# A fused Hyena filter and maxout FFN: the w_out product two steps behind, and another load table for the VectorE work between

## The chip, the cores and the metric

One core of a Trainium2 chip runs the whole kernel. The metric is device time in microseconds of one execution; several executions of each kernel are timed, and the median is compared. The engines of the core run side by side, each with its own in-order queue, and wait for each other by semaphores: TensorE (PE, matmuls; PEld its weight loads), VectorE (DVE), ScalarE (ACT), GpSimd (POOL) and SyncE (SP, which here issues DMAs only).

## The reference

A long convolution (by FFT) along the sequence, gated by the input, and then a feed-forward block whose hidden value is the maximum of three products:

```python
def _attn_ref(x, v, pos_emb, w1, w2):
    B, S, D = x.shape                                  # 4, 12544, 128
    h_mlp = np.maximum(pos_emb @ w1, 0.0) @ w2
    h_filt = h_mlp * np.exp(-0.01 * pos)[:, None]
    u = x * v
    L = 2 * S
    Uf = np.fft.rfft(u, n=L, axis=1)
    Hf = np.fft.rfft(h_filt, n=L, axis=0)
    y = np.fft.irfft(Uf * Hf[None], n=L, axis=1)[:, :S, :]
    return x * y

def _moe_ref(x, w1, w2, w3, w_out):                    # x: 50176 x 128, d_ff 768
    h = np.maximum(np.maximum(x @ w1, x @ w2), x @ w3)
    return h @ w_out
```

All of it is float32.

## The kernel before

The convolution of one batch is a three-stage transform made of small matmuls; the FFN of one batch takes its result from DRAM. A prologue computes the filter's spectrum and the first batch's convolution. Then comes the loop that the change touches: while the FFN of batch b runs (b = 0, 1, 2), the convolution of batch b+1 is spread between its steps. A last part does the FFN of batch 3 alone, in another form.

*The FFN.* A batch is 32 tiles (`NT`) of 392 columns, and d_ff is 6 steps (`NF`) of 128 rows. w1 has been subtracted from w2 and w3 beforehand, and its part is applied as one 128x128 matrix `lin`, so that step f of a tile is: `up` (L689) makes `pa = w_sb[1]ᵀ g`, ScalarE writes `hid = relu(pa)` (L694), `pb = w_sb[2]ᵀ g`, and VectorE writes `hid = max(hid, pb)` (L697). `down` (L700) adds `wo_sb[f]ᵀ hid` into the accumulator `ops`; in step 0 it first starts that accumulator with `lin`, in step 5 ScalarE copies it to `ot` (L710) and POOL issues the output DMA (L712). Each of `pa`, `pb`, `lin` and one `ops` product is four matmul instructions on two column halves of the array.

Buffers: `pa` and `pb` take turns through three PSUM banks (`hps`, 3 buffers); `ops` is one bank; `hid` has 3 buffers, `ot` 2, `gt` 3.

*The next tile.* `t_load` (L634) loads its transformed data `zt` and the gate `xT`, two tiles ahead. `t_sums` (L658) makes a sum and a difference, in step 1: on POOL (L662, L663), but on VectorE (two L666) for tiles of the upper half of batches 1 and 2. `t_last` (L670), in step 3, does the last transform stage (`yps`) and the gating (`gt`, L684).

*The convolution between.* `conv_steps` (L572) hands out its work to the 192 slots (32 tiles of 6 steps) of a batch's FFN. For u in 0..31 come loads, a product, a transpose and the first stage (`u_first`). Then 45 pairs of frequencies (`NK`) go through the middle: products with 64x64 weights (`g_quarter`, `psq`, L462 and L472, in slot s; it also does the third stage of the pair three before, from its `xs`), `g_fold` in slot s+1 (ScalarE copies half of `psq` to `eo`, L484, VectorE adds and subtracts, L487), `q_swap` in s+2 and s+3 (two ScalarE copies each, L502, L503), then `q_re` (VectorE, L506), `q_im` (VectorE L511, then POOL L514) and two `q_unfold` (VectorE, L518) in the slots that `emptiest` picks by the table `load`, and at the end `g_store` (POOL DMA, L495). `per_pair`, the distance of two pairs, is 2.67 slots in the first batch and 2.53 in the others, so the pairs fall differently on the six steps of a tile.

*The order.* Nothing reorders: the program's order is each engine's order. Within one step the loop emits `t_load` (step 0), `t_sums` (step 1), `up` of this step, `down` of the step before, `t_last` (step 3), and then what `conv_steps` put into the slot; `q_swap`, `g_fold` and the rest in the order of their pairs, `g_quarter` and `u_first` last. So `ot` of a tile stands, on ScalarE, after the first activation of the next tile and ahead of the swaps and the fold of its slot 0; on POOL its output DMA stands ahead of the next `t_sums`.

Of the kernel before, what the change touches and what calls it, by code (L numbers as in the profile page):

```python
# [89 lines left out]
def kernel(  # L90
# [59 lines left out]
    def halves_mm(out, lhsT, rhs, start, stop):  # L150


        for h in range(2):
            nc.tensor.matmul(out[64 * h:64 * h + 64], lhsT[:, 64 * h:64 * h + 64], rhs,  # L154
                             start=start, stop=stop, skip_group_check=True)
# [416 lines left out]
    def conv_steps(b, done):  # L572


        out = []

        def at(slot, late, fn, *args):
            out.append((slot, late, len(out), fn, args))

        per_pair = 170 / (NK + LATE + 0.6 * (NU - done))
        for u in range(done, NU):
            s = (u - done) * 0.6 * per_pair + 9
            at(max(0, int(s) - 9), 0, u_load, b, u)
            at(int(s) - 6, 0, u_mul, u)
            at(int(s) - 5, 0, u_planes, u)
            at(int(s) - 4, 0, u_dma, u)
            at(int(s), 0, u_join, u)
            at(int(s + 1), 1, u_first, u)  # L590
        s0 = int((NU - done - 1) * 0.6 * per_pair + 9) + 6
        load = [(1.2 if i % NF == 3 else 0.6) + (1.4 if i % NF == 1 and b > 1 and i >= NT * NF // 2 else 0)
                for i in range(NT * NF)]
        for x in range(NK + LATE):
            load[s0 + int(x * per_pair) + 1] += 1.4

        def emptiest(among, cost):
            s = min(among, key=lambda i: load[i])
            load[s] += cost
            return s  # L600

        for x in range(NK + LATE):
            s = s0 + int(x * per_pair)
            g, z = x if x < NK else None, x - LATE if x >= LATE else None
            at(s, 1, g_quarter, g, z)
            at(s + 1, 0, g_fold, g, z)
            at(s - 4, 0, w_load, x)
            if z is not None:
                at(s + 3, 0, g_store, b, z)
            if g is None:  # L610
                continue
            if g % 2 == 0:
                at(s - 4, 0, q_load, g, min(2, NK - g))
                at(s - 1, 0, h_load, g, min(2, NK - g))
            at(s + 2, 0, q_swap, g, 0)
            at(s + 3, 0, q_swap, g, 64)
            last = s0 + int((x + LATE) * per_pair) - 1
            a = emptiest(range(s + 4, min(s + 5, last - 2) + 1), 0.7)
            at(a, 0, q_re, g)
            a = emptiest(range(a, min(s + 6, last - 1) + 1), 0.7)  # L620
            at(a, 0, q_im, g)
            for q in range(2):
                at(emptiest(range(a + 1, last + 1), 0.55), 0, q_unfold, g, q)
        slots = {}
        for s, _, _, fn, args in sorted(out, key=lambda r: r[:3]):
            slots.setdefault(s, []).append((fn, args))
        return slots
# [6 lines left out]
    def t_load(b, i):  # L634
        zt = hp.tile([N1, 2, 512], FP32, tag="zt", name="zt", bufs=2)
        for c in range(2):
            if b == 0:
                nc.sync.dma_start(
                    zt[NK * c:NK * c + NK],
                    zd[b].rearrange("(g a) c t f -> g a c t f", a=2)[  # L640
                        :, :, c, 2 * i:2 * i + 2, :].rearrange("g a t f -> g a (t f)"))
                continue
            q, j = divmod(i, NT // 2)
            for a in range(2):
                nc.sync.dma_start(
                    zt[NK * c:NK * c + NK, a].rearrange("g (t f) -> g t f", t=2),
                    zd[b].rearrange("(g a) c t q f -> g a c t q f", a=2)[
                        :, a, c ^ (a & q), 2 * j:2 * j + 2, q, :])
        zts[b, i] = zt[:, 0], zt[:, 1]
        if i % 2:  # L650
            return
        xT = hp.tile([D, 2, 4, NB], FP32, tag="xT", name="xT", bufs=2)
        for c in range(GC):
            nc.sync.dma_start(xT[c * NG:(c + 1) * NG].rearrange("d i p n -> d (i p) n"),
                              x[:, 4 * i:4 * i + 8, c, b, :])
        xTs[b, i], xTs[b, i + 1] = xT[:, 0], xT[:, 1]

    def t_sums(i, eng=nc.gpsimd):  # L658
        z0, z1 = zts[i]
        even = hp.tile([N1, 512], FP32, tag="even", name="even", bufs=2)  # L660
        if i[0] == 0 or i[1] < NT // 2:
            eng.tensor_tensor(out=even[:], in0=z0, in1=z1, op=ALU.add)  # L662
            eng.tensor_tensor(out=z1, in0=z0, in1=z1, op=ALU.subtract)  # L663
        else:
            for out, op in ((even[:], ALU.add), (z1, ALU.subtract)):
                nc.vector.scalar_tensor_tensor(out=out, in0=z1, scalar=sign_t[:, 0:1], in1=z0,  # L666
                                               op0=ALU.mult, op1=op)
        zts[i] = even[:], z1

    def t_last(i):  # L670
        zt = zts.pop(i)
        ps = cps.tile([P, state["yps"]], FP32, tag="cv", name="yps")
        own = i[0] == B - 1 and i[1] > 1
        g = (lp if own else hp).tile([D, 4, NB], FP32, tag="g", name="gt", bufs=4 if own else 3)
        y = ps[:, 0:N].rearrange("d (p n) -> d p n", p=4)

        h = NB // 2
        for s in range(4):
            for a in range(2):
                halves_mm(y[:, s, a * h:a * h + h], zt[a][:, s * D:(s + 1) * D],  # L680
                          f4p[:, i[0] > 0 and i[1] >= NT // 2, a, :], s == 0 and a == 0, True)
        y = y.rearrange("d p (a m) -> d p m a", a=2)
        xT = xTs.pop(i)
        nc.vector.tensor_tensor(out=g[:].rearrange("d p (m a) -> d p m a", a=2), in0=y,  # L684
                                in1=xT.rearrange("d p (m a) -> d p m a", a=2),
                                op=ALU.mult)
        gs[i] = g
# [12 lines left out]
    def down(i, f, h):  # L700
        if f == 0:
            pos_[i] = ops.tile([D, 512], FP32, tag="ops", name="ops")
            halves_mm(pos_[i][:, 0:N], lin[:], gs[i][:].rearrange("d p n -> d (p n)"), True,
                      False)
        halves_mm(pos_[i][:, 0:N], wo_sb[:, f, :], h[:], False, f == NF - 1)
        if f < NF - 1:
            return
        gs.pop(i)
        o = op_.tile([D, 4, NB], FP32, tag="o", name="ot")
        nc.scalar.copy(o[:].rearrange("d p n -> d (p n)"), pos_.pop(i)[:, 0:N])  # L710
        dst = outT.rearrange("d (p b n) -> d p b n", b=B, n=NB)[:, 4 * i[1]:4 * i[1] + 4, i[0], :]
        nc.gpsimd.dma_start(dst, o[:])  # L712
# [94 lines left out]
    def run(steps):  # L807
        for fn, args in steps:
            fn(*args)
# [216 lines left out]

    tiles = [(b, i) for b in range(B) for i in range(NT)]
    LAST = (B - 1) * NT
    late = None
    for n, (b, i) in enumerate(tiles[:LAST]):  # L1030
        if i == 0:
            beside = {}
            beside = conv_steps(b + 1, EARLY if b == 0 else 0)
        if n == 0:
            t_load(*tiles[0])
            t_load(*tiles[1])
            t_sums(tiles[0], nc.vector)
            t_last(tiles[0])
        for f in range(NF):

            if i < NT - 2:
                if f == 0:
                    t_load(*tiles[n + 2])
            elif i == NT - 1 and f < 2 and n + 1 + f < len(tiles):
                t_load(*tiles[n + 1 + f])
            turn_ = i == NT - 1
            if f == (3 if turn_ else 1):
                t_sums(tiles[n + 1], nc.vector if turn_ else nc.gpsimd)
            if f == 4 and n + 1 == LAST:
                t_sums(tiles[n + 2], nc.vector)  # L1050
            h = up((b, i), f)
            if late is not None:
                down(*late)
            late = ((b, i), f, h)
            if f == (4 if turn_ else 3):
                t_last(tiles[n + 1])
            if f == 5 and n + 1 == LAST:
                t_last(tiles[n + 2])
            s = i * NF + f
            run(beside.pop(s, ()))  # L1060
            if s == NT * NF - 1:
                assert not beside, sorted(beside)
    first = up((B - 1, 0), 0)
    down(*late)
    conv.close()


# [20 lines left out]
    step, b = 0, B - 1  # L1088
    for i in range(0, NT, 2):
        h = {}  # L1090
# [63 lines left out]
```

## Time and profile before

| | us |
|---|---|
| median of 6 runs | 2351.21 |
| lowest and highest | 2348.91, 2354.92 |
| the profiled execution, its time | 2354.92 |
| its span, first to last instruction | 2353.1 |

Granted TensorE clock over the span: 0.994 of full speed. Busy time by stretch, in us, with the DMA engines' share (packet times over 16 engines, which can exceed 1):

| stretch | what runs | PE | DVE | ACT | POOL | DMA |
|---|---|---|---|---|---|---|
| 0 to 340 | prologue, first convolution | 316.8 | 235.6 | 219.9 | 108.5 | 0.72, 0.82 |
| 340 to 990 | FFN of batch 0 and some of 1 | 648.0 | 436.0 | 333.8 | 279.2 | 0.90 |
| 990 to 1460 | FFN of batch 1 and some of 2 | 461.7 | 325.1 | 255.4 | 158.5 | 0.88 |
| 1460 to 1930 | FFN of batch 2 | 461.5 | 332.9 | 258.2 | 159.9 | 0.86 |
| 1930 to 2353 | FFN of batch 3 | 412.4 | 198.4 | 105.2 | 268.4 | 0.22 |

A line of a list of groups or waits reads: line of the kernel, engine, operation, written<-read tiles. In a timeline, each row is a run of equal instructions: start, length, engine, line, operation, tiles, how many, and in brackets the engine's idle time before it and what ended it. The end of a matmul is modelled, so rows of TensorE overlap; the distance of starts is the safer measure.

### The profile page before, as it was taken

How to read it: one execution, taken by the hardware profiler on the slowest of the kernel's cores; microseconds unless marked ns; L12 is line 12 of the kernel's file. 1: busy time of each engine (PE TensorE's matmuls, PEld its weight loads, DVE VectorE, ACT ScalarE, POOL GpSimd, SP SyncE). 2: the span in 40 equal slices, each digit the busy share in tenths (PEclk: the TensorE clock that was granted, in tenths of full speed). 3: DMA queues.
4: the chain of work that ended last, by engine and by line, in shares of the span. 5: the costliest groups of instructions: out<-in, count | busy, mean ns of one | idle time of the engine just before them, and what ended most of it. 6: DMA issues, size and time to landing. Idle time of an engine off the chain costs nothing.

```text
span 2353.1 us, 67998 instructions
## 1 busy us (share of the span) xinstructions
PE 2300.4 (98%) x27853; PEld 1374.3 (58%) x27853; DVE 1528.1 (65%) x2798; ACT 1172.4 (50%) x2124; POOL 974.6 (41%) x1153
## 2 busy tenths in 40 slices
PE   8999989999999999999999999999999999999998
PEld 7988866655545446654454446655454546666665
DVE  4678857757777747757787747757777755444443
ACT  2678844456666624446666624446666622222222
POOL 1045414334444434334332324434333326666666
PEclk9999999999999999999999999999999999999999
DMA  6868959979898859979989849969899932222221
GB/s 149 209 201 263 288 148 186 167 175 229 224 241 218 209 124 191 185 142 239 229 233 239 223 111 194 185 145 243 223 228 244 228 81 70 57 54 66 68 54 22
DMA packets 473145, 410.92 MB, mean 175 GB/s; under 512 B 328004, under 2 KB 374231, under 8 KB 472834
## 3 DMA queue, kind: packets, MB, share of 16 engines
q1 hardware_dynamic: 433504, 317.61, 61.2%
q0 software_dynamic: 26400, 75.72, 11.1%
q10 hardware_dynamic: 12930, 13.25, 1.8%
q8 instruction: 219, 3.59, 0.7%
q14 instruction: 92, 0.75, 0.1%
HBM read 262.77 MB, written 84.67 MB: 148 GB/s over the span
## 4 chain that ended last, share of the span: by engine, by line
PE 80%; DMA 8%; ACT 4%; issue 3%; DVE 3%; SPq 1%; POOL 1%; ACTq 0%; POOLq 0%; DVEq 0%
PE pa L154 20%; PE pb L154 19%; PE ops L154 16%; PE ops L757 6%; PE ps L408 5%; PE yps L154 5%; PE psq L462 3%; PE ps L163 3%; PE psq L472 2%; DMA hd<-ht 2%; DMA wt<-wq_const 1%; DMA zt<-zd 1%; DMA sq<-spec 1%; ACT ht L949 1%; PE pm L323 1%
## 5 line engine op out<-in xcount | busy, mean ns | idle before, releaser
L694 ACT ACTIVATE hid<-pa 128x392 f32<-128x392 f32 x768 | 383.1, 499 | 683.5 <-PE pa L154 658.0
L697 DVE TENSOR_TENSOR hid<-hid,pb 128x392 f32<-128x392 f32 x768 | 428.3, 558 | 425.5 <-PE pb L154 332.3
L154 PE MATMUL pa<-gt,w_sb 128*64 128x392 f32 x3072 | 648.3, 499 | 0.8 <-DVE gt L684 0.8
L154 PE MATMUL pb<-gt,w_sb 128*64 128x392 f32 x3072 | 638.9, 493 | 3.7 <-ACT hid L694 3.7
L154 PE MATMUL ops<-hid,wo_sb 128*64 128x392 f32 x2304 | 478.9, 493 | 15.6 <-DVE hid L697 15.6
L154 PEld LDWEIGHTS pb<-gt,w_sb 128*64 128x64 f32 x3072 | 223.4, 137 | 288.2 <-issue 270.8
L514 POOL TENSOR_TENSOR cb<-cb,xs 128x512 f32<-128x512 f32 x135 | 174.7, 1294 | 445.2 <-DVE xs L511 167.7
L154 PEld LDWEIGHTS ops<-hid,wo_sb 128*64 128x64 f32 x2304 | 165.8, 137 | 232.5 <-issue 169.2
L154 PEld LDWEIGHTS pa<-gt,w_sb 128*64 128x64 f32 x3072 | 196.3, 137 | 137.7 <-issue 93.2
L712 POOL DMA_DIRECT2D out_dram<-ot x96 | 74.4, 775 | 420.0 <-ACT ot L710 296.8
L502 ACT ACTIVATE xs<-cb 32x512 f32<-32x512 f32 x270 | 169.5, 628 | 111.4 <-DVE cb L487 107.2
L487 DVE TENSOR_TENSOR cb<-psq,eo 128x512 f32<-128x512 f32 (+1 forms) x288 | 175.1, 649 | 72.4 <-ACT eo L484 72.4
L419 DVE TENSOR_TENSOR spec<-ps,high 128x360 f32<-128x360 f32 (+1 forms) x204 | 141.9, 738 | 116.7 <-ACT high L417 116.4
L503 ACT COPY xs<-cb 32x512 f32<-32x512 f32 x270 | 166.3, 616 | 3.1
L417 ACT COPY high<-ps 128x360 f32<-128x360 f32 (+1 forms) x102 | 77.2, 761 | 170.3 <-PE ps L408 112.7
L408 PEld LDWEIGHTS ps<-f1q,uT 98*64 98x64 f32 x3072 | 132.3, 137 | 35.0 <-issue 32.5
L154 PEld LDWEIGHTS yps<-f4p,even 90*64 90x64 f32 x2048 | 116.5, 139 | 41.3 <-issue 36.2
L408 PE MATMUL ps<-f1q,uT 98*64 98x90 f32 x3072 | 136.7, 241 | 3.6 <-DVE spec L419 2.6
L684 DVE TENSOR_TENSOR gt<-yps,xT 128x392 f32<-128x392 f32 x128 | 72.5, 566 | 98.5 <-PE yps L154 58.5
L154 PE MATMUL yps<-f4p,even 90*64 90x49 f32 x2048 | 125.7, 221 | 3.6 <-DMA f4p<-f4p_const 3.6
L154 PE MATMUL yps<-f4p,zt 90*64 90x49 f32 x2048 | 127.4, 223 | 0.0
L518 DVE TENSOR_TENSOR xs<-cb 128x256 f32<-128x256 f32 x270 | 115.9, 468 | 3.7 <-POOL cb L514 3.2
(130 smaller groups left out, 3340.8 us busy)
## 6 DMA issues: line engine op xcount, KB each, us to landing
ht<-hd SPq DMA_DIRECT2D x264, 256.0 KB, 5.9
wt<-wq_const SPq DMA_DIRECT2D x144, 256.0 KB, 6.8
zd<-cb POOLq DMA_DIRECT2D x135, 256.0 KB, 6.1
zt<-zd SPq DMA_DIRECT2D x384, 90.0 KB, 3.2
sq<-spec SPq DMA_DIRECT2D x264, 128.0 KB, 7.1
ut<-in_xr_dram SPq DMA_DIRECT2D x128, 196.0 KB, 4.1
ut<-in_vr_dram SPq DMA_DIRECT2D x128, 196.0 KB, 4.4
xT<-in_x_dram SPq DMA_DIRECT2D x256, 98.0 KB, 4.3
```

The costliest lines, as they stand in the source:

```text
L154: nc.tensor.matmul(out[64 * h:64 * h + 64], lhsT[:, 64 * h:64 * h + 64], rhs, start=start, stop=stop, skip_group_check=True)
L408: nc.tensor.matmul(ps[64 * c:64 * c + 64, 256 * i + h * N1:256 * i + (h + 1) * N1], t[:, 2 * ((at + i) % 8) + h].rearrange("n r t -> n (r ...
L417: nc.scalar.copy(high, v[:, 0])
L419: nc.vector.tensor_tensor(out=spec[:, :, a, at:at + n], in0=v[:, 1], in1=high, op=op)
L487: nc.vector.tensor_tensor(out=cb[:, a, lo:hi], in0=ps[:, lo:hi], in1=eo[:, lo:hi], op=op)
L502: nc.scalar.mul(xs[at:at + 32], xt[at + 32:at + 64], -1.0)
L503: nc.scalar.copy(xs[at + 32:at + 64], xt[at:at + 32])
L514: nc.gpsimd.tensor_tensor(out=xts[g], in0=xts[g], in1=xs[:], op=ALU.add)
L518: nc.vector.tensor_tensor(out=ab[:, q], in0=y[:, 0], in1=y[:, 1], op=(ALU.subtract, ALU.add)[q])
L694: nc.scalar.activation(h[:], pa[:, 0:N], Relu)
L697: nc.vector.tensor_tensor(out=h[:], in0=h[:], in1=pb[:, 0:N], op=ALU.max)
L757: nc.tensor.matmul(ps[64 * c:64 * c + 64, 0:H2], w, rhs[:, H2 * c:H2 * c + H2], start=start, stop=True, skip_group_check=True)
```

## The change

Three things. In the main loop `late` becomes a list: `down` is emitted when three steps are waiting, so that the product with `w_out` runs two steps after its `up` and not one. After the loop, the two that are left are emitted behind the first `up` of batch 3. And in `conv_steps` the table `load`, by which `emptiest` picks slots for `q_re`, `q_im` and `q_unfold`, gets 1.2 less in each slot that has a `g_quarter`; the slot after it has 1.4 more, as before.

```diff
         for x in range(NK + LATE):
-            load[s0 + int(x * per_pair) + 1] += 1.4
+            s = s0 + int(x * per_pair)
+            load[s] -= 1.2
+            load[s + 1] += 1.4
...
-    late = None
+    late = []
...
             h = up((b, i), f)
-            if late is not None:
-                down(*late)
-            late = ((b, i), f, h)
+            late.append(((b, i), f, h))
+            if len(late) > 2:
+                down(*late.pop(0))
...
     first = up((B - 1, 0), 0)
-    down(*late)
+    for l in late:
+        down(*l)
     conv.close()
```

## The prediction

> **What bounds the kernel.** I read the busy shares first, then the list of waits, then the lengths of matmul groups in the timeline, and last the other engines around one long wait.
>
> ```profile
> PE 2300.4 (98%) x27853; PEld 1374.3 (58%) x27853; DVE 1528.1 (65%) x2798; ACT 1172.4 (50%) x2124; POOL 974.6 (41%) x1153
> ```
>
> TensorE (PE) is busy for 98% of the span, and by stretches (340 to 990, 990 to 1460, 1460 to 1930) the time in which the first three batches go through the FFN leaves it idle for 2.0 + 8.3 + 8.5 = 18.8 us. So whatever TensorE no longer waits for there comes off the end, and nothing else does. The list of waits says for what it waits (total us, times, longest):
>
> ```profile
> PE ops L154 <- DVE hid L697: 15.6, 13, 1.8
> PE pb L154 <- ACT hid L694: 3.7, 1, 3.7
> PE psq L472 <- DVE xs L518: 0.8, 3, 0.4
> PE psq L462 <- DMA zt<-zd: 0.6, 2, 0.5
> PE psq L462 <- DMA wt<-wq_const: 0.6, 1, 0.6
> PE psq L462 <- DMA sq<-spec: 0.4, 1, 0.4
> ```
>
> The first line is the one that the change touches: `down` waits for the maximum (L697) that VectorE writes. One of these 13 waits, in the timeline of TensorE, then VectorE, then ScalarE (start, us, engine):
>
> ```profile
> 1114.03 0.83 PE L154 MATMUL pa<-gt,w_sb 128*64 128x392 f32 x4
> 1114.69 0.83 PE L154 MATMUL pb<-gt,w_sb 128*64 128x392 f32 x4
> 1115.35 0.83 PE L154 MATMUL ops<-gt,lin 128*64 128x392 f32 x4
> 1116.01 0.83 PE L154 MATMUL ops<-hid,wo_sb 128*64 128x392 f32 x4
> 1116.66 0.83 PE L154 MATMUL pa<-gt,w_sb 128*64 128x392 f32 x4
> 1117.32 0.83 PE L154 MATMUL pb<-gt,w_sb 128*64 128x392 f32 x4
> 1119.90 0.88 PE L154 MATMUL ops<-hid,wo_sb 128*64 128x392 f32 x4 [1.75 <-DVE hid L697]
> ```
> ```profile
> 1116.65 1.29 DVE L487 TENSOR_TENSOR cb<-psq,eo 128x512 f32<-128x512 f32 x2 [2.43 <-ACT eo L484]
> 1117.86 0.74 DVE L666 SCALAR_TENSOR_TENSOR even<-zt,sign 90x512 f32<-90x512 f32 x1
> 1118.63 0.75 DVE L666 SCALAR_TENSOR_TENSOR zt<-zt,sign 90x512 f32<-90x512 f32 x1
> 1119.30 0.55 DVE L697 TENSOR_TENSOR hid<-hid,pb 128x392 f32<-128x392 f32 x1
> ```
> ```profile
> 1114.25 0.48 ACT L710 COPY ot<-ops 128x392 f32<-128x392 f32 x1 [0.82 <-PE ops L154]
> 1114.76 0.63 ACT L502 ACTIVATE xs<-cb 32x512 f32<-32x512 f32 x1
> 1115.39 0.61 ACT L503 COPY xs<-cb 32x512 f32<-32x512 f32 x1
> 1116.03 0.58 ACT L484 COPY eo<-psq 128x512 f32<-128x512 f32 x1
> 1116.52 0.50 ACT L694 ACTIVATE hid<-pa 128x392 f32<-128x392 f32 x1
> ```
>
> Read backwards: `down` of step 1 (1119.90) waits for the maximum of step 1 (ends 1119.85). That stands behind the two sums of the next tile's `t_sums` and behind the fold (L487). The fold waits for `eo`, `eo` stands behind two swaps, and these behind the copy `ot`, for which ScalarE sat 0.82 us idle until `down` of the old tile's last step was done. A group of `pa`, `pb` or `ops` costs 0.66 us from start to start (1116.66 to 1117.32).
>
> **The change, part by part.**
>
> *The wait removed.* From `pb` to `ops` above are 2.58 us instead of 0.66: 1.92 lost, where the list says 1.75, as a group's modelled end lies 0.17 behind the next start. Over 13 waits 15.6 + 13 × 0.17 = 17.8 us. By kind: eight of 1.92 (15.4), four in each of the second and third batch where the `t_sums` of the upper half are on VectorE; and five small ones of about 0.48 (2.4) in the first batch (`pb` 526.17, `ops` 527.31).
>
> *Where the stall goes.* The next to need that maximum is `pa` of step 3: three banks serve `pa` and `pb` in turn, and the first one of step 3 is the bank of step 1's `pb`, which L697 reads. In the new order the matmuls from 1114.03 on run: `up` 1 (1.32, to 1115.35), `down` of the old step 5 (0.66, 1116.01), `up` 2 (1.32, 1117.33), `lin` and `down` 0 (1.32, 1118.65), the products `psq` (1.19 from the end of `ops` to the next `pa`, as after 1119.90), so `pa` 3 at 1119.84. With VectorE exactly as late as now, 1119.85, about 0.1 us is left at each of the eight: 0.8 at most. But VectorE will be earlier. `ot` now follows the activation of step 1, so swaps and `eo` start when the first activation ends (1113.43 instead of 1114.76), 1.3 us earlier, and the fold with them. I take nothing left. The small waits end at 527.26, and their `pa` 3 would come at 528.5: nothing left.
>
> `pb` 2 is the other consumer to look at: it needs the activation of step 1, which ends at 1117.02 now and would be wanted at 1116.67. By the same 1.3 us it comes in time; without that cover it would cost 0.35 × 13 = 4.6.
>
> *What is moved.* All counts are equal; 96 copies `ot` (485 ns) and 96 output DMAs (POOL issues of 0.78) go one FFN step later. On ScalarE what queues behind `ot` are now the swaps and fold copies of step 1 and the activation of step 2, for which `pb` 3 waits. The worst tiles (swap and fold in step 1, three in each later batch) have 0.48 + 0.63 + 0.62 + 0.58 + 0.50 = 2.8 us of ScalarE from the start of `ot`, while TensorE takes 0.66 × 5 = 3.3 from the end of `down` to `pb` 3. `lin` of the next tile waits for `ot`, as `ops` is one bank; the way there is one `up`, 1.32, before and after. Nothing: at 84 of 96 places ScalarE was already there, idle until `ops` was done (66.0 us in all). A third buffer of `hid` was there already; the activation of step f overwrites what `down` f-3 read, and that stands ahead of it on TensorE. SP's queue keeps its order.
>
> *POOL.* The output DMA was in front of the `t_sums` (L662, L663: 1.29 and 1.27) and held them until `ot` was done; now it comes behind, so they start up to some 3 us earlier, 61 times. This has a price on VectorE: L511 takes 682 ns in the median and 1760 at most, each long one beside an L663; L518 417 and 2219. So a meeting costs VectorE 1.1 to 1.8 us. It reaches TensorE where a `q_unfold` of step 0 or 1 is read by the products one step later. I count 15 such tiles in the first batch and two in each of the others. At the longest wait of today, 0.4, that is 7.6; the other end is -0.8, today's three waits gone. Today's collisions move away as new ones come, so I take +0.5.
>
> The Trainium skill (GPSIMD Engine Reference, Specifications) says that POOL shares its SBUF interfaces with VectorE and contends with VectorE instructions that have two SBUF inputs; L511 and L518 are of that kind. Taken alone it would charge every moved `t_sums` that meets one, and speaks against this change; the rows show that most meetings stay hidden, and by them I price it.
>
> *The spread of VectorE work.* By the formulas of `conv_steps`, old and new, seven of the steps of 135 pairs move, each by one slot: `q_re` 0 of the first batch, and `q_re` 31, `q_im` 24 and 43 in both others. Each is 0.68 us of VectorE, so at most 7 × 0.68 = 4.8 either way. None is in a tile of the 13 waits, and the maximum now has at least 2.64 us of matmuls as cover (four groups) before anyone wants it. I take 0; this part of the change does next to nothing.
>
> *Transfers.* TensorE comes to its loads up to 1.9 us earlier per tile. Today's waits for DMA are 1.6 us in all, with DMA engines 93 to 95% busy where the long waits are. SP is mostly held by consumers (147.4 us for the `ht` buffers until L511), which move along. Ends: -1.6 (they vanish) to +15.4 (all gain of the later batches is eaten, a rival below); I take +1.0, nearer to today's row.
>
> *The end of the loop.* Two `down` follow the first `up` of the last batch instead of one, but the same matmuls lie before the last `ot`; the 3.7 us of `pb <- ACT hid`, which wait for its output DMA, stay.
>
> **Sum.** -17.8 + 0 + 0.5 + 0 + 1.0 = -16.3 us. The profiled execution took 2354.9 (2353.1 of span and 1.8 around it), the slowest of six; it would take 2338.6. Against the median 2351.2 this is **2335**.
>
> **The rivals.** A, transfers set the pace of the second and third batch: for it speaks the DMA share of 0.93 to 1.05 there; against it, that TensorE waits 1.6 us for DMA in all and is busy without a gap through whole stretches with a share above 1.0 (900 to 980 us). Only the 2.4 us of the first batch go: 2349. 7%.
>
> B, the wait changes its name: VectorE, pushed about by the earlier `t_sums`, is late for `pa` 3 or for the products. 0.8 left and 7.6 for the products: -17.8 + 8.4 = -9.4, 2342. 10%.
>
> C, slower: `ot` late for `lin`. In front of `ot` now also stand step 0's swaps and fold, 0.63 + 0.62 + 0.58 = 1.83 us, in the 24 tiles that have a fold in step 0. If ScalarE had no slack there, `lin` would wait 24 × 1.83 = 43.9, the time would be 2351.2 - 17.8 + 43.9 = 2377; it is slower by over 0.2% from 0.94 us per tile on. Against: ScalarE's work to there is 0.50 + 1.83 + 0.50 = 2.83 us from the first activation, TensorE's 3.96 from the first `pa`. 5%.
>
> That the change doesn't do what it says, because `pa` 3 would have waited anyway: it does want the same maximum, and this holds as far as it comes before 1119.85; by the sum above it comes 0.01 us before that. Counted in B.
>
> **Numbers.** The forecast has 78%, A 7, B 10, C 5. The range: below, -17.8 - 0.8 - 1.6 = -20.2 and 2.3 for the spread of the six runs (2348.9 to 2351.2): 2329. Above, B with 3.7 of spread upwards (2354.9): 2346. It holds the forecast and B and leaves out A and C, 12%, and some of the edges. Within 0.2% (4.7 us, about what a measurement of this kernel can tell from no change) is A's case: faster 0.88, same 0.07, slower 0.05.
>
> **What would show it.** Right: no wait of `ops` for L697 among TensorE's waits, `ot` behind the second activation of a tile, the tiles that take 17.84 us from first `pa` to first `pa` (1112.01 to 1129.85) down by 1.9. Wrong: a line `pa <- DVE hid` or `psq <- DVE xs` of several us (B), more than 5 us of TensorE for DMA (A), `ops <- ACT ot` (C).

## The result and the profile after

The changed kernel takes 2345.8 us in the median of 19 runs (2336.84 to 2354.01); the kernel before, run beside it, 2352.7 (42 runs, 2348.25 to 2362.0). The ratio is 0.9971, with a 95% interval of 0.9963 to 0.9979: 6.8 us or 0.29% faster. The forecast was 16.3 us.

The profiled execution took 2343.64 us. Its engines' busy times are those of before within 4 us, but POOL's is 11 us less:

```profile
span 2341.8 us, 68062 instructions
...
PE 2298.6 (98%) x27853; PEld 1378.0 (59%) x27853; DVE 1524.2 (65%) x2798; ACT 1174.1 (50%) x2124; POOL 963.4 (41%) x1153
```

The list of TensorE's waits (us in total, times, longest) has changed. The 15.6 us for the maximum are gone; `pb <- ACT hid` has 7 entries where it had one, and `psq` waits longer for DMA and for the unfold (the kernel's lines are two higher behind the load table of `conv_steps`):

```profile
PE pb L154 <- ACT hid L696: 7.4, 7, 3.8
PE psq L462 <- DMA wt<-wq_const: 4.8, 3, 3.1
...
PE psq L472 <- DVE xs L518: 1.5, 2, 1.0
...
PE pa L154 <- DVE gt L686: 0.7, 1, 0.7
```

The tile whose long wait was shown of before, in the timelines of TensorE, VectorE and ScalarE (start, us, engine, line, operation, tiles):

```profile
1112.81 0.83 PE L154 MATMUL ops<-hid,wo_sb 128*64 128x392 f32 x4
1113.47 0.83 PE L154 MATMUL pa<-gt,w_sb 128*64 128x392 f32 x4
1114.13 0.83 PE L154 MATMUL pb<-gt,w_sb 128*64 128x392 f32 x4
1114.79 0.83 PE L154 MATMUL ops<-gt,lin 128*64 128x392 f32 x4
1115.45 0.83 PE L154 MATMUL ops<-hid,wo_sb 128*64 128x392 f32 x4
1116.20 0.67 PE L462 MATMUL psq<-sq,wt 64*64 64x128 f32 x16
1116.69 0.62 PE L472 MATMUL psq<-xs,wt 64*64 64x128 f32 x16
1117.24 0.88 PE L154 MATMUL pa<-gt,w_sb 128*64 128x392 f32 x4
1117.95 0.83 PE L154 MATMUL pb<-gt,w_sb 128*64 128x392 f32 x4
```
```profile
1112.81 1.29 DVE L487 TENSOR_TENSOR cb<-psq,eo 128x512 f32<-128x512 f32 x2 [1.13 <-ACT eo L484]
...
1115.46 0.55 DVE L699 TENSOR_TENSOR hid<-hid,pb 128x392 f32<-128x392 f32 x1
1115.93 0.75 DVE L518 TENSOR_TENSOR xs<-cb 128x256 f32<-128x256 f32 x2
```
```profile
1112.19 0.59 ACT L484 COPY eo<-psq 128x512 f32<-128x512 f32 x1
1112.67 0.51 ACT L696 ACTIVATE hid<-pa 128x392 f32<-128x392 f32 x1
1113.69 0.48 ACT L712 COPY ot<-ops 128x392 f32<-128x392 f32 x1 [0.51 <-PE ops L154]
```

TensorE goes through without a gap: from `pa` at 1113.47 to the next at 1117.24 there are three more groups and the products, and nothing waits. `ot` now stands behind the activation of step 1, so `eo` no longer waits for it, the fold starts when TensorE has reached `ops` at 1112.81, and the maximum ends at 1116.01, 1.23 us before the `pa` of step 3. In the built program, which names the bank of every tile, that `pa` takes the bank of step 2's `pa`, not the one that this maximum reads; the bank of step 1's `pb` is overwritten by the `pb` at 1117.95, so there are 1.9 us to spare. What comes closest is the products: the second of the two unfolds behind the maximum ends at 1116.68, and the half of `psq` that reads it starts at 1116.91, behind a weight load that waits for it until 1116.80. The tile takes 15.87 us instead of 17.84.

Where the rest went shows when the loop is measured tile by tile, from first `pa` to first `pa`, in both profiles. The loop over the first three batches takes 1590.56 us before and 1582.33 after (batches: 521.40, 534.78, 534.38 against 521.83, 530.69, 529.81). TensorE is busy for 1572.5 us of it before and 1571.5 after, so its idle time falls from 18.1 to 10.9.

| what | where | us |
|---|---|---|
| waits for the maximum, removed | batch 0, tiles 11, 15, 19, 23, 27: 0.54 each; batches 1 and 2, tiles 15, 18, 23, 26: 1.98 each | -18.5 |
| the three waits of the products for an unfold, removed | batch 0, tile 23: 0.61; tile 12 of batches 1 and 2: 0.35 and 0.34 | -1.3 |
| `pb` waits for its own step's activation | tile 1 of each batch, 1.64 | +4.9 |
| VectorE slowed beside POOL's sums | batch 0: tiles 12, 16, 20, 24, 28 0.30 each, 2, 6, 30 1.44 together; batches 1 and 2: tile 8 0.33 each; batch 2 tile 13 1.22 | +4.8 |
| loads late for the products | batch 1, tiles 20 to 22 2.9; batch 2, tile 20 0.63; less 0.62 in batch 1, tile 11, where the kernel before waited for loads | +2.9 |
| the rest | tile 0 of batch 0 -0.81, others -0.26 together | -1.1 |

That is -8.3 by tiles, -8.2 by the ends of the loop. Most of tile 0's -0.81 is no gain: with `down` a step later, one product of 0.66 us runs behind the first `pa` of batch 3 and so outside the loop as measured here; the part behind the loop takes 428.89 us instead of 427.95. Together that is -7.3, and the difference to the 6.8 us of the medians is small beside what the prologue does by chance: with equal instructions it takes 328.9 to 334.6 us in the profiles of this study.

*The first cost.* Tile 1 of batch 1 in the changed kernel, TensorE and then ScalarE:

```profile
865.90 0.83 PE L154 MATMUL pa<-gt,w_sb 128*64 128x392 f32 x4
867.33 0.88 PE L154 MATMUL pb<-gt,w_sb 128*64 128x392 f32 x4 [0.60 <-ACT hid L696]
868.03 0.83 PE L154 MATMUL ops<-hid,wo_sb 128*64 128x392 f32 x4
868.69 0.83 PE L154 MATMUL pa<-gt,w_sb 128*64 128x392 f32 x4
870.12 0.88 PE L154 MATMUL pb<-gt,w_sb 128*64 128x392 f32 x4 [0.60 <-ACT hid L696]
```
```profile
866.78 0.50 ACT L696 ACTIVATE hid<-pa 128x392 f32<-128x392 f32 x1 [1.48 <-PE pa L154]
...
869.57 0.50 ACT L696 ACTIVATE hid<-pa 128x392 f32<-128x392 f32 x1 [2.29 <-PE pa L154]
```

Read it from `pa` to `pb`: 1.43 us from start to start instead of 0.66 (869.46 to 870.12 at this place in the kernel before), and in between lies the activation of the same step, which ends at 867.28; `pb` starts right behind it. So `pb` writes the bank that its own `pa` was in. In the built programs this is so for none of 768 `pb` groups before and for exactly six after: steps 0 and 1 of tile 1 of each of the three batches. The pool of three buffers doesn't go round there. Nor did it go round before: of the 1536 groups of `pa` and `pb`, 56 take a bank that one of the two groups ahead of them had, each of them a `pa`; after the change 69 do, and six of these are a `pb`.

*The second cost.* Tile 12 of batch 0, VectorE and then POOL, first in the kernel before, where the tile starts at 537.20:

```profile
539.32 0.75 DVE L518 TENSOR_TENSOR xs<-cb 128x256 f32<-128x256 f32 x2
```
```profile
540.23 0.78 POOL L712 DMA_DIRECT2D out_dram<-ot  x1 [1.03 <-ACT ot L710]
541.02 1.29 POOL L662 TENSOR_TENSOR even<-zt 90x512 f32<-90x512 f32 x1
```

And in the changed kernel, where it starts at 534.08:

```profile
536.21 2.88 DVE L518 TENSOR_TENSOR xs<-cb 128x256 f32<-128x256 f32 x2
539.01 1.27 DVE L487 TENSOR_TENSOR cb<-psq,eo 128x512 f32<-128x512 f32 x2
```
```profile
536.02 1.36 POOL L664 TENSOR_TENSOR even<-zt 90x512 f32<-90x512 f32 x1
537.46 1.34 POOL L665 TENSOR_TENSOR zt<-zt 90x512 f32<-90x512 f32 x1
539.08 0.80 POOL L714 DMA_DIRECT2D out_dram<-ot  x1 [0.28 <-ACT ot L712]
```

Two unfolds take 2.88 us where they took 0.75. They run from 0.2 us after the start of POOL's first sum to 0.3 after the end of its second, and TensorE's `psq` of this slot, which reads them, is 0.30 late. The output DMA, which in the kernel before held the sums back until the unfolds were done, now stands behind them. In the whole trace 39 unfolds overlap one of POOL's sums, where there were 15 before. The old meetings did go: VectorE's multiplication in `q_im` (L511) took up to 1760 ns beside a sum before and 686 at most now.

*The third cost.* SyncE's queue before a wait in batch 1, and TensorE at its end:

```profile
1199.31 1.20 SPq L423 DMA_DIRECT2D wt<-wq_const  x2
1200.56 5.39 SPq L433 DMA_DIRECT2D sq<-spec  x4
```
```profile
1205.39 0.83 PE L154 MATMUL ops<-hid,wo_sb 128*64 128x392 f32 x4
1209.34 0.67 PE L462 MATMUL psq<-sq,wt 64*64 64x128 f32 x16 [3.12 <-DMA wt<-wq_const]
```

The weights issued at 1199.31 landed at 1209.21, 9.9 us later (7.3 us is the median of this load), and the product that wants them starts there, 3.12 us late.

### The profile page after: what moved, and what is told of

It is laid out like the page before. It is cut to its first block, busy times and chain, and to the rows that moved or that the text cites. A ratio compares the mean times of both kernels' runs of the same rounds, so it can differ in the third digit from the quotient of the medians.

```text
span 2341.8 us, 68062 instructions
## 1 busy us (share of the span) xinstructions
PE 2298.6 (98%) x27853; PEld 1378.0 (59%) x27853; DVE 1524.2 (65%) x2798; ACT 1174.1 (50%) x2124; POOL 963.4 (41%) x1153
## 3 DMA queue, kind: packets, MB, share of 16 engines
q0 software_dynamic: 26400, 75.72, 11.4%
## 4 chain that ended last, share of the span: by engine, by line
PE 86%; DMA 4%; ACT 3%; issue 3%; DVE 2%; ACTq 0%; POOL 0%; SPq 0%; POOLq 0%; DVEq 0%
PE pa L154 21%; PE pb L154 20%; PE ops L154 17%; PE ops L759 6%; PE ps L408 5%; PE yps L154 5%; PE psq L462 3%; PE ps L163 3%; PE psq L472 2%; DMA hd<-ht 2%; ACT ht L951 1%; PE pm L323 1%; DVE xs L518 1%; DMA wt<-wq_const 1%; PE pst L361 1%
## 5 line engine op out<-in xcount | busy, mean ns | idle before, releaser
L514 POOL TENSOR_TENSOR cb<-cb,xs 128x512 f32<-128x512 f32 x135 | 174.2, 1290 | 495.8 <-ACT xs L503 190.9
L518 DVE TENSOR_TENSOR xs<-cb 128x256 f32<-128x256 f32 x270 | 134.9, 538 | 7.6 <-POOL cb L514 6.6
L377 POOL COPY planes<-ut 128x784 uint16<-128x784 uint16 x90 | 75.7, 842 | 132.3 <-DVE ut L356 129.4
```

The lines of the kernel that those rows point to most:

```text
L514: nc.gpsimd.tensor_tensor(out=xts[g], in0=xts[g], in1=xs[:], op=ALU.add)
L518: nc.vector.tensor_tensor(out=ab[:, q], in0=y[:, 0], in1=y[:, 1], op=(ALU.subtract, ALU.add)[q])
```

## The experiments

All were timed in five rounds beside the kernel before, in three sessions (median of before 2353.29, 2349.2 and 2352.39 us); ratios are to the kernel before of the same session. "The loop" is the length from the first `pa` to that of batch 3 in the run's profile. The theory after the result: the lag does all, its 19 us are there, and three costs give most of them back. Rivals: the load table costs the missing part, or the later batches are bound by transfers.

**The lag alone, and the table alone.** e1 is the changed kernel with the old table:

```diff
-            s = s0 + int(x * per_pair)
-            load[s] -= 1.2
-            load[s + 1] += 1.4
+            load[s0 + int(x * per_pair) + 1] += 1.4
```

> The new lag with the old load table. Theory (the lag does it all, the table nothing): 0.997 of before, as the whole change, within 0.001; no wait of ops for the maximum; six waits of pb for the activation of its own step, in steps 0 and 1 of the second tile of each batch, 0.77 us each. Rival (the table gave some of the gain back, or made some of it): at least 0.002 away from the whole change in one direction.

Measured: 2343.5 us, ratio 0.9955 (0.9941 to 0.9969), 0.0016 below the whole change, between the theory's 0.001 and the rival's 0.002; loop 1584.89. No wait of `ops` for the maximum is left, and tile 1 is 1.63, 1.64 and 1.63 longer in the three batches:

```profile
PE pb L154 <- ACT hid L694: 7.2, 7, 3.7
```

e2 has the new table and the old lag:

```diff
             h = up((b, i), f)
-            late.append(((b, i), f, h))
-            if len(late) > 2:
-                down(*late.pop(0))
+            if late is not None:
+                down(*late)
+            late = ((b, i), f, h)
...
```

> The old lag with the new load table. Theory: no change, 1.000 within 0.001, the 13 waits of ops for the maximum stay, some 17.8 us in all. Rival (the table has a price of its own): 1.001 to 1.002, up to 4.8 us.

Measured: 2354.27 us, ratio 1.0005 (0.9995 to 1.0015); loop 1590.45, and the wait stays:

```profile
PE ops L154 <- DVE hid L699: 15.6, 13, 1.8
```

The lag brings the gain and also the six waits of `pb`; the table does neither.

**The banks in a fixed turn.** e3 is the whole change, with the three banks as fixed tiles, taken in turn:

```diff
-    hps = ctx.enter_context(tc.tile_pool(name="hps", bufs=3, space=PSUM))
+    hps = ctx.enter_context(tc.tile_pool(name="hps", bufs=1, space=PSUM))
+    ring = [hps.tile([P, 512], FP32, name=f"hb{i}") for i in range(3)]
...
-        pa = hps.tile([P, 512], FP32, tag="hps", name="pa")
+        pa = ring[0]
...
-        pb = hps.tile([P, 512], FP32, tag="hps", name="pb")
+        pb = ring[1]
+        ring.append(ring.pop(0))
+        ring.append(ring.pop(0))
```

> The whole change, and the three banks of pa and pb as three tiles taken in a fixed turn, so that no pb can get the bank of its own step's pa. Theory (the allocator's choice of bank costs 6 x 0.77 = 4.6 us): the six waits of pb in the second tile of each batch are gone, that tile is 1.6 us shorter in each batch, and the ratio is 0.002 below the whole change: 0.995. Rival (the activation is late there for another cause, or the transfers take what is gained): waits stay or come elsewhere, 0.997.

Measured: 2339.13 us, ratio 0.9939 (0.9926 to 0.9951); loop 1577.31, 5.0 less than with the change as it is. TensorE at the place shown above (`pa` and `pb` are both called `hb` here, and make one row):

```profile
865.54 0.83 PE L154 MATMUL ops<-hid,wo_sb 128*64 128x392 f32 x4
866.19 1.49 PE L154 MATMUL hb<-gt,w_sb 128*64 128x392 f32 x8
867.51 0.83 PE L154 MATMUL ops<-hid,wo_sb 128*64 128x392 f32 x4
```

From `ops` to `ops` 1.97 us, three groups of 0.66: the wait is gone, as are the extra 1.64 us of all three tiles. That the banks cost 4.9 us is shown by these tiles; that the loop as a whole is 5.0 shorter is partly chance, as others differ too (the 1.22 of tile 13 in batch 2 are gone here with the sums still on POOL, and late loads moved). e5 puts the same turn into the kernel before, as a control:

> The old lag and the old table, with the fixed turn of the three banks alone. Theory (the allocator's order was already the fixed turn before the change, so the turn only mends what the lag broke): 1.000 within 0.001, the 13 waits for the maximum stay. Rival (the fixed turn is faster by itself): 0.998.

Measured: 2352.97 us, ratio 1.0015 (1.0005 to 1.0024); loop 1591.41; the 13 waits of 15.6 us are there. So the turn itself gains nothing (it is slightly above the band expected, for which there is no explanation), and what e3 gains over the change is the mishap that the change met. The theory's reason was wrong, though: the allocator's order before was no fixed turn, but its 56 other choices cost nothing.

e6 is e3 with the old table:

> New lag, fixed turn, old load table. Theory (the table does nothing that can be measured): 0.994 as with the new table, within 0.001. Rival (the new table costs 2 to 4 us): 0.992 to 0.993.

Measured: 2338.93 us, ratio 0.9961 (0.9948 to 0.9974), outside the band expected; loop 1580.26, where 5.7 us are waits of the products for DMA. With and without the new table the ratios are 0.9971 and 0.9955 under the pool, 0.9939 and 0.9961 under the turn: of opposite sign, so no effect of the table that these runs can tell. (In the profiles the loop is 2.6 and 3.0 us longer with the old table, mostly in late loads; one profile of each doesn't settle that.)

**POOL's sums.** e4 is e3 with the sums that go to POOL emitted behind `down`, so that the output DMA is in front of them again:

```diff
+            on_pool = not turn_ and not (b and i + 1 >= NT // 2)
-            if f == (3 if turn_ else 1):
-                t_sums(tiles[n + 1], nc.vector if turn_ else nc.gpsimd)
+            if f == (3 if turn_ else 1) and not on_pool:
+                t_sums(tiles[n + 1], nc.vector)
...
                 down(*late.pop(0))
+            if f == 1 and on_pool:
+                t_sums(tiles[n + 1], nc.gpsimd)
```

> As the kernel with the fixed turn, and where the two sums of the next tile are on POOL they are emitted after down, so that the output DMA stands ahead of them again as it did before the change. Theory (the earlier sums meet VectorE's unfolds ahead of the products): the waits of psq for xs shrink to under 1 us, the tiles 12, 16, 20, 24 and 28 of the first batch lose 0.3 us each again, and the ratio is another 0.001 lower: 0.994. Rival (the meetings cost nothing, the rest is transfers): no change against the fixed turn, within 0.0005.

Measured: 2342.7 us, ratio 0.9949 (0.9935 to 0.9962); loop 1581.95. The 0.3 us of tiles 12, 16, 20, 24 and 28 and the 0.8 of tile 30 went, but against the kernel before tiles 13, 17, 21, 25 and 29 of batch 0 are 1.0 to 1.2 longer and tile 11 of the others 0.74 and 0.94, and TensorE has a new wait:

```profile
PE psq L462 <- DVE cb L487: 2.1, 2, 1.0
```

The meetings did become fewer; the group of unfolds is back at the busy time of before, but its idle time, the third figure, has grown from 7.2 us in e3 to 22.5:

```profile
L518 DVE TENSOR_TENSOR xs<-cb 128x256 f32<-128x256 f32 x270 | 115.8, 468 | 22.5 <-POOL cb L514 21.9
```

The output DMA is itself one step later than before the change, so the sums behind it are a step later than they were, and now hold up POOL's own next work, the addition of `q_im` (L514), for which the unfolds wait. In tile 13 of batch 0 the sums run from 555.06 to 557.71, that addition follows until 558.94, and VectorE sits idle for 2.35 us before its unfolds at 558.98. So the ratio is no test of the meetings; what e4 shows is that late sums have a price of their own.

e7 takes POOL out of it: all sums on VectorE, everywhere in the loop.

```diff
-                t_sums(tiles[n + 1], nc.vector if turn_ else nc.gpsimd)
+                t_sums(tiles[n + 1], nc.vector)
```

> New lag, fixed turn, and the two sums of the next tile on VectorE in all tiles, so that POOL's SBUF work does not meet VectorE's there. Theory (meetings stretch VectorE's unfolds): the mean of an unfold falls from about 0.54 us to 0.42, the tiles 12, 16, 20, 24, 28 of the first batch lose their 0.3 us, tile 30 its 0.8; the loop is 2 to 3 us shorter than with the fixed turn alone, if the 1.4 us per tile on VectorE are covered: 0.993. Rival (VectorE is then late by itself): new waits of psq or pa for VectorE, 0.995 or more.

Measured: 2334.75 us, ratio 0.9939 (0.9927 to 0.9951), not the 0.993 expected, and nothing that the medians can tell from e3; loop 1573.93, 3.4 less than in e3. The 0.30 of the five tiles, the 0.82 of tile 30, and those of tiles 2 and 6 and of tile 8 in the later batches are gone; tiles 4, 5 and 8 of batch 0 are 0.25 to 0.33 longer, and one new wait of the products, 0.9, is put down to VectorE (L511). VectorE at the same work as in tile 12 above:

```profile
533.52 0.76 DVE L518 TENSOR_TENSOR xs<-cb 128x256 f32<-128x256 f32 x2
534.19 1.28 DVE L487 TENSOR_TENSOR cb<-psq,eo 128x512 f32<-128x512 f32 x2
535.39 0.68 DVE L664 TENSOR_TENSOR even<-zt 90x512 f32<-90x512 f32 x1
536.10 0.69 DVE L665 TENSOR_TENSOR zt<-zt 90x512 f32<-90x512 f32 x1
```

The two unfolds take 0.76 us instead of 2.88, and the sums 1.37 instead of 2.70. Over the whole kernel the group of unfolds reads (busy us, mean ns of one, then the idle time before it), before, after and in e7:

```profile
L518 DVE TENSOR_TENSOR xs<-cb 128x256 f32<-128x256 f32 x270 | 115.9, 468 | 3.7 <-POOL cb L514 3.2
```
```profile
L518 DVE TENSOR_TENSOR xs<-cb 128x256 f32<-128x256 f32 x270 | 134.9, 538 | 7.6 <-POOL cb L514 6.6
```
```profile
L518 DVE TENSOR_TENSOR xs<-cb 128x256 f32<-128x256 f32 x270 | 102.2, 418 | 7.2 <-POOL cb L514 6.5
```

The change adds 19 us to 270 unfolds, and without POOL's sums 33 go, the longest unfold being 426 ns: the slow unfolds are the meetings.

**Transfers.** e8 is e3 without the loads of the gate in 47 of 48 pairs of tiles (18.9 MB less):

```diff
+        if 0 < b < B - 1 or b == 0 and i:
+            xTs[b, i], xTs[b, i + 1] = xTs["kept"]
+            return
...
+        xTs["kept"] = xT[:, 0], xT[:, 1]
```

> New lag, fixed turn, and the loads of the gate xT are left out in the first three batches but for the first pair of tiles (48 x 4 loads of 98 KB less; the output of these batches is gated by the wrong values). Theory (about 3 us of what was given back are transfers that come too late for the products): the waits of psq for DMA fall under 1 us in all, the loop is 2 to 4 us shorter than with the fixed turn alone, 0.992 to 0.993. Rival (these waits come from the order of the loads and their buffers, not from the amount moved): the waits stay, 0.994.

Measured: 2332.49 us, ratio 0.993 (0.9918 to 0.9942); loop 1571.88, 5.4 less than e3 and more than expected, with 0.6 us of the products' waits for DMA left. e10 does the same to e7:

> New lag, fixed turn, sums on VectorE, and the gate loads of the first three batches left out but for the first pair of tiles (these batches are gated by the wrong values). Theory (bank, meetings and transfers are all that was given back, and they add): the loop of the first three batches is 1570 us within 2, some 20 us less than before the change, ratio 0.991. Rival (something else limits the loop): 1574 or more, as with the gate loads.

Measured: 2330.11 us, ratio 0.9905 (0.9891 to 0.9918); loop 1569.87, both as expected, 4.1 less than e7. What is left of the products' waits for DMA:

```profile
PE psq L462 <- DMA wt<-wq_const: 1.4, 2, 0.9
```

e9 leaves all loads in, and only issues the weights two slots earlier, into one buffer more:

```diff
-        w = wp.tile([P, 2, 2, 2, 64], FP32, tag="w", name="wt")
+        w = wp.tile([P, 2, 2, 2, 64], FP32, tag="w", name="wt", bufs=4)
...
-            at(s - 4, 0, w_load, x)
+            at(s - 6, 0, w_load, x)
```

> New lag, fixed turn, sums on VectorE, and the 64x64 weights loaded six slots ahead of their product and not four, into four buffers and not three. Theory (the late weights are bursts behind other loads, and two slots, some 5 us, cover the longest wait of 3 us): no wait of psq for wt over 0.5 us, 1 to 3 us less than with the sums on VectorE alone, 0.992 to 0.993. Rival (the transfers as a whole are at their limit there): the wait takes another name, sq, ht or zt, and the ratio stays at 0.994.

Measured: 2332.01 us, ratio 0.9911 (0.9898 to 0.9925); loop 1567.95, 6.0 less than e7. No product waits for DMA any more, with the same 410.9 MB moved and the DMA engines as busy (0.91 to 0.92, 206 GB/s) in the later batches. Of the 6.0 us, twice the most that was expected, the waits for DMA that e7 lists explain 3.8; the 0.9 put down to L511 is gone too, with nothing but the loads changed. So it isn't the amount that the transfers can't carry; the loads were issued too late. e9 beats both kernels: 20.4 us under the kernel before in its session. TensorE is busy for 1567.6 of the 1568.0 us of its loop, so no wait is left there to be removed.

## Why the prediction was right and wrong

*The waits removed: right.* 13 waits went, 18.5 us where 17.8 were counted; the eight long ones were worth 1.98 and not 1.92, the small ones 0.54 and not 0.48. The path to them (maximum, sums, fold, `eo`, swaps, `ot`) was the right one.

*The stalls moved to `pa` 3, `pb` 2 and `lin`: right at nothing, though for `pa` 3 not for the reason given.* The maximum is there 1.23 us before `pa` 3 in the tile shown, but in step 3 of all eight tiles with the long wait `pa` takes the bank of step 2's `pa`, before and after, and doesn't need that maximum; TensorE's waits have no line of `pa` for `hid`, and none of `ops` for `ot`. Rival C is out. The end-of-loop wait of `pb` stayed, 3.8 us for 3.7.

*"Three banks serve `pa` and `pb` in turn": wrong, and this is the step that failed.* It was taken from three buffers and two users, and carried the sum's zero for "where the stall goes". The waits of before didn't speak against it (no `pb` waited for its own activation), but they showed what the allocator's choice cost in that order of work, not a rule that it keeps; the built program of before already breaks the turn at 56 places, at no cost. With `down` one step later the pool gave a `pb` the bank of its own `pa` at six places, 4.9 us, and e3 takes them back. Why it did so there is open: that it picks a buffer by its own estimate of when one comes free is only a guess.

*POOL: the mechanism was right, the size was not.* Earlier sums, meetings with VectorE, a price at the products: that is what e7 shows. But the term was 0.5 and measured 3.5 (4.8 of new delays, in 11 tiles and not 19, less the 1.3 of today's three waits, which did go), inside the bounds of -0.8 to 7.6. What failed is that "today's collisions move away as new ones come" was taken as an even exchange. In VectorE's time it was one (L511 7.6 us less, the unfolds 19.0 more, all its work together 3.9 less). But L511 is not what TensorE waits for next, and the unfolds are. The old order had the output DMA as a gate, which happened to keep the sums off many of the unfolds; the sums now start while the tile's first unfolds run.

*Transfers: right in kind, too small.* 1.0 was taken and 2.9 measured, in one profile: the products' waits for DMA are 4.8 us there, 4.7 in e1, 3.8 in e3 and 5.7 in e6, against 1.6 before. The reason given, that TensorE comes to its loads earlier, fits: the late loads of batch 1 are in tiles 20 to 22, behind the waits removed in tiles 15 and 18. Rival A, a pace set by transfers, is out, as e9 moves the same bytes without a wait; it is the lead of the issue that was sized to the old pace.

*The table: right at nothing*, by e2 and as far as both pairs of ratios can tell.

Sum: the -16.3 of the forecast was -7.2 by the terms it names (-18.5, 4.9 for the banks where it had 0, 3.5 and 2.9), which is also by how much TensorE's idle time in the loop fell, and -6.8 in the medians. So of 9.1 us missed the banks are 4.9, POOL 3.0 and the transfers 1.9, and 0.7 more were gained than counted. With the banks in turn (e3) the ratio of 0.9939 is 14.4 us, and -18.5 + 3.5 + 2.9 = -12.1 is what the terms leave when the banks' 4.9 go: the forecast's working, with its two small costs as measured.

The range, 2329 to 2346, holds the measured 2345.8 by 0.2 us. That is luck: its upper end was rival B's 2342 with the spread of the runs, and B named the wrong waits (`pa` for the maximum, 0.8) beside the right one (the products for the unfold). As a change, B's -9.4 is the nearest to the measured -6.8 (as a time A's 2349 is, since the kernel before took 1.5 us more beside the changed one than its 2351.21), though half of its reason didn't happen, and the banks, the largest cost, are in none of the rivals.

## What to carry to other kernels

A pool with n buffers isn't a ring: when consumers are shifted, look in the built program at which release each write waits for, or fix the order by hand where it matters. An instruction that waits in a queue is a gate for what stands behind it; take it away, and price what then runs earlier by whom it meets, not by the meetings of today. When stalls go, loads whose lead was just enough for the old pace come late: give them depth in the same edit.

## What the runs showed of the hardware

A VectorE operation with two SBUF inputs beside a POOL `tensor_tensor` is not slowed by a share, but nearly stands until POOL's sum is over: two unfolds that take 0.75 us alone took 2.88, the time of the two sums of 1.36 and 1.34 with little more. In the changed kernel's trace all 30 unfolds of over 0.7 us end 0.28 to 0.29 us after the end of one of POOL's sums. Operations with one of their two inputs in PSUM show nothing of it there: the 52 maxima that overlap a sum take 554 ns in the median, as the others do, and the 27 operations of the fold 681 against 680. The Trainium skill (GPSIMD Engine Reference, Specifications) names this pair, POOL and VectorE instructions with two SBUF inputs, as contending for SBUF interfaces that they share; the runs agree, with a mean of 468 ns before, 538 after and 418 without the sums on POOL.

DMA engines 0.91 busy were no limit in e9; from 1180 to 1210 us the share was 1.05, and TensorE was busy without a gap. In the changed kernel, from 1180 to 1210 us at a share of 0.96, the load of the weights, 7.3 us in the median over the kernel, took 9.9. Under such a load a single transfer's time is spread widely (2.6 to 11.4 us for this one), and the lead must cover the spread and not the median.
